# Another written order for the first part of an attention and two-MLP kernel

## The chip, the cores and the metric

The kernel runs on one core of a Trainium2 chip. The metric is the device time of one execution in microseconds (us). A core has five engines with instruction queues of their own: PE (matrix products; the load of its weights is shown as PEld), DVE (vector), ACT (functions such as exponential and sine), POOL (general purpose) and SP, whose queue issues the DMA transfers here. Each engine takes its queue strictly in order and waits on semaphores for the others.

## The reference, cut to what matters

```python
# attention: 4 batches, 8 heads, 576 positions, 64 columns
q_d, k_d, v_d = means of q, k, v over 4 neighbouring positions
out_d = softmax(scale * q_d @ k_d.T) @ v_d           # repeated 4 times
scores = scale * q @ k.T, only where |i - j| < 4     # a band of 7
x = repeat(out_d, 4) + softmax(scores) @ v           # -> 2304 x 512
# first MLP, d_ff 2048
h = x @ w_in;  y = (h * cos(h)) @ w_out
# second MLP, d_ff 1536
out = ((y @ w_a) * (y @ w_b)) @ w_out2
```

All is 32-bit floating point. The kernel splits each operand of a large product into a high and a low part and adds three products.

## The kernel before

The kernel has two parts. The first holds the attention, the first MLP and the preparation of the second MLP's weights; the second part is the second MLP. The change lies in the first part.

The 2304 positions are cut into eight half sequences u of 288. For each u the attention runs in two pairs of heads, pr 0 and 1. Its steps have short names, which the order and all the text below use with u and pr or a head pair behind: sm adds four neighbours of q and k (down_sums, L379, nine adds on POOL for sm0.x by sum4, L370, three reductions on DVE); lp and dp are the local and down-sampled scores on PE; lm is mask and row maximum on DVE; lu subtracts the maximum (L415); le and de are the exponentials on ACT (L442, L449); ln and dn the sums; lz and dz the scaling by them (L464, L486, on ACT L484); lt and dt the transposes on PE, lc and dc the copies behind them (L290, L292); da is the negation and maximum of the down-sampled scores (L436, L438); vp adds v on PE, vq copies it; at is the product with v; up and cb put both results together into x; xh and xl split x into its high and low part.

The first MLP follows block by block. hG.c are the matmuls of group G (one block of 128 hidden columns for one u) into PSUM for chunk c; cG.0 to cG.5 are six steps of h cos h (cosine, L653): c.0 on ACT, c.1 on DVE, c.2 the sine on ACT (L660), c.3 the product on DVE (L662), which also sets the PSUM buffer free, c.4 the copy of the high part and c.5 the low part (L668); bG.m are the matmuls back (three each, mm3, L587 to L589). wK.0 to wK.4 convert the K-th weight block (L266, L269, L271, L290 or L292, L580). Loads are L0.. for the first tensors and then Lq, Lk, Lv, Lw (sums of v, tile vs) and LcK (weight block K, L261); pN.0 is a load for the second MLP (praw).

What sets the order is one string, ORDER (L51 to L159), with 2320 words. Each word is a task; a letter behind @ names the engine (a ACT, d DVE, p POOL) where more than one can do it. The loop at L972 takes word after word and writes the task's instructions; the class InOrder (L175) then fixes for every engine that it keeps the written order. So a task's place in the string is its place in its engine's queue, and a load's place is its place in SP's queue. Buffers are few: att is one PSUM buffer, h is two, q tiles three; groups 2 and 3 use accumulators (EARLY). A load of a q tile waits until the tasks that read the buffer's last content are done, and everything behind it in SP's queue waits too. ACT holds one function table at a time: exponential and sine need different ones, and the build puts a table load (ACT_TABLE_LOAD, shown under the line of the instruction behind it) where the written order goes from one to the other.

Of the kernel before, what the change touches and what calls it, by code (L numbers as in the profile page):

```python
# [55 lines left out]
sm1.1@d Lc10 vq0.2@a ln0.1 lz0.1@d vq0.3@a Lc8 h0.0 w6.2@d h1.0 w9.1@a dz0.2@p dt0.1 dc0.1@a w3.0@a h1.1 Lq2.0 lt0.1 lc0.10@a lc0.11@a at0.1 w5.2@d
h2.0 h2.1 w6.3@d w10.1@a w9.2@d w3.1@a up0.1@d cb0.2 xh0.2@a cb0.3 w6.4@p w3.2@d h0.1 L0w7 sm1.0@d xh0.3@a xl0.3@d w8.1@a lp1.0 xl0.2@p h2.2 h1.2
w3.3@d h0.2 h0.3 w8.0@a w4.3@a w8.2@d w7.1@a lm1.0 c0.0@a w3.4@p Lc12 w4.4@p c0.1@d Lc15 Lk2.1 h1.3 c1.0@a c1.1@d Lc26 w7.0@a w7.2@d w7.3@d Lq1.2
w5.3@d h2.3 c2.0@a h3.0 h3.1 c0.2@a Lc13 h3.2 h3.3 c3.0@a dp1.0 c1.2@a dx1.0 w7.4@p Lq1.3 lu1.0@p c0.3@d da1.00@d c1.3@d lu1.1@d h5.0 h5.1 h5.2
da1.01@d sm1.2@d lp1.1 sm1.3@d w5.4@p c2.1@d Lk2.0 h4.0 Lc16 w12.0@a c0.4@d c1.4@d c1.5@p Lc27 w10.0@a w12.1@a w8.3@d Lc11 h4.1 lm1.1 h4.2 c0.5@p b0.1  # L60
w9.3@a h5.3 w10.2@d lu1.2@p le1.0 ln1.0 lz1.0@p de1.0 dn1.0 b0.0 Lc30 c2.2@a c3.1@d c2.3@d h4.3 dp1.1 dx1.1 da1.10@d w11.1@a c4.0@a Lc29 da1.11@d b1.0
lu1.3@p b0.3 b1.3 w8.4@d b1.1 dz1.0@p lt1.0 lc1.00@d lc1.01@d c3.2@a c3.3@d w9.4@d c2.4@a w13.0@a c2.5@p b2.0 b2.1 le1.1 dz1.1@p c3.4@d c3.5@p w15.1@a
dt1.0 ln1.1 dc1.0@a w10.3@a sm2.0@d b2.3 b0.2 w10.4@p b1.2 at1.0 b3.0 up1.0@d Lq2.1 c4.1@d w11.0@a cb1.1 c5.0@a b2.2 de1.1 b3.1 cb1.0 b3.3 dn1.1
lz1.1@p lt1.1 b3.2 c4.2@a Lw2.0 w11.2@d Lc18 lc1.11@a lc1.10@a Lc14 w11.3@a dz1.3@p sm2.1@d lp2.0 xh1.1@a c4.3@d c5.1@d lm2.0 vs2.0@p w15.0@a Lc24
xl1.1@d xh1.0@a w11.4@p h6.0 h6.1 Lc22 c4.4@a Lq2.2 dz1.2@p c5.2@a c5.3@d h6.2 Lc20 w14.1@a h6.3 c6.0@a w13.1@a lu2.1@p dt1.1 Lc19 dc1.1@d c5.4@a
c6.1@d w12.2@d c4.5@d h7.0 w14.0@a w12.3@a h7.1 at1.1 up1.1@a w14.2@d cb1.2 cb1.3 Lc25 c6.2@a c6.3@d h7.2 h7.3 c7.0@a xh1.2@a xh1.3@a xl1.0@p dp2.0
Lc21 w12.4@p b4.3 w13.2@d Lw2.1 Lk2.3 h8.0 w19.0@a b4.0 c7.1@d c7.2@a dx2.0 Lq2.3 c7.3@d w13.3@a h8.1 w20.1@a w20.0@a xl1.2@p h8.2 da2.00@d xl1.3@p
w15.2@d da2.01@d h9.0 h9.1 Lk2.2 h9.2 w27.0@a h9.3 vs2.1@p c6.4@a Lq3.0 lp2.1 c5.5@p h8.3 b4.1 w25.0@a w13.4@d b5.3 b5.1 sm2.3@d c6.5@p lm2.1 w14.3@a
w14.4@p Lc23 b4.2 b5.2 Lc17 b5.0 b6.0 lu2.0@p lu2.2@p c8.0@a c8.1@d w16.0@a Lc28 sm2.2@d c9.0@a c9.1@d b6.3 w24.0@a dp2.1 c8.2@a c8.3@d c7.4@d b6.1
lu2.3@p h10.0 w15.3@a w15.4@p dx2.1 da2.10@d h10.1 h10.2 c9.2@a le2.0 b6.2 Lv2 Lq3.2 da2.11@d h10.3 de2 c10.0@a c9.3@d c7.5@p b7.2 b7.0 ln2.0 Lw2.2  # L70
vs2.2@p h11.0 b7.1 le2.1 Lq3.1 lz2.0@p h11.1 c10.1@d c10.2@a dn2 h11.2 h11.3 c11.0@a c8.4@a c10.3@d b7.3 e7.0@d sm3.1@p e7.3@d lt2.0 dz2.0@p lc2.01@a
c11.1@d dz2.1@p h12.0 h12.1 h12.2 lc2.00@a dt2.0 Lw2.3 c8.5@p ln2.1 e7.2@a vs2.3@p c11.2@a c11.3@d c9.4@d h12.3 b8.2 dc2.0@a at2.0 w20.2@d up2.0@d
c12.0@a c12.1@d c9.5@p h13.0 w24.1@a w30.1@a S7.0 h13.1 c11.4@a lz2.1@p cb2.1 h13.2 h13.3 b8.0 b9.0 S7.2 c10.4@a c10.5@p sm3.0@d cb2.0 Lw2.4 vs2.4@p
w26.1@a e7.1@a c13.0@a S7.3 dp3.0 w24.2@d b8.1 b9.2 c13.1@d p1.0 dx3.0 da3.00@d da3.01@d c12.2@a w22.0@a b8.3 b9.3 b10.3 c13.2@a xh2.0@a lp3.0 xh2.1@a
c12.3@d Lw2.5 w20.3@a w16.1@a c13.3@d h14.0 h14.1 h14.2 w26.0@a w21.1@a c12.4@d dz2.3@a lm3.0 w16.2@d w30.0@a dz2.2@p h14.3 w20.4@p h15.0 lt2.1
lc2.10@a h15.1 lc2.11@d c14.0@a c11.5@d xl2.1@p w17.1@a w21.0@a h15.2 sm3.2@d h15.3 c15.0@a w24.3@d dt2.1 dc2.1@d lu3.1@p b9.1 Lq3.3 sm3.3@d c13.4@d
c12.5@d b10.1 c14.1@d b10.2 vs2.5@p Lq4.1 at2.1 b11.1 up2.1@d c15.1@d b10.0 w22.1@a c13.5@p cb2.2 w27.1@a b11.0 c14.2@a cb2.3 w17.0@a xh2.3@a b12.1
c14.3@d w27.2@d lu3.0@p b12.0 S7.1 lp3.1 xl2.3@d p1.11 Lk4.0 xh2.2@a xl2.0@p h16.0 lm3.1 w18.0@a b11.3 c15.2@a c15.3@d w22.2@d Lk4.1 c14.4@a xl2.2@p
w24.4@p le3.0 h16.1 b13.1 h16.2 dp3.1 dx3.1 w23.1@a c15.4@d da3.11@d da3.10@d h17.0 h17.1 Lv3 h17.2 h17.3 ln3.0 c14.5@p b14.1 c15.5@p w23.0@a b11.2
h16.3 w23.2@d c17.0@a de3 c17.1@d Lq4.3 b12.3 b13.3 b14.3 c16.0@a lz3.0@p c16.1@d w18.1@a dn3 c17.2@a b13.0 b14.0 b15.0 Lq4.0 w21.2@d lt3.0 c17.3@d  # L80
b12.2 lc3.01@a e15.0@a c16.2@a sm4.0@d b15.1 e15.1@a c16.3@d b13.2 b14.2 b15.2 e15.2@a w30.2@d lu3.2@p lc3.00@a b15.3 h19.0 w29.0@a h19.1 e15.3@a
h19.2 h19.3 c19.0@a c17.4@d Lw4.0 dz3.0@p S15.0 S15.2 sm4.1@d c16.4@a dz3.1@p dt3.0 dc3.0@a c19.1@d lu3.3@p h18.0 h18.1 c17.5@p h18.2 w17.2@d w19.1@a
at3.0 up3.0@d c16.5@p c19.2@a le3.1 vs4.0@p c19.3@d h18.3 b16.2 dz3.3@p h20.0 b16.3 cb3.1 Lw4.1 cb3.0 w19.2@d ln3.1 lz3.1@p c18.0@a c18.1@d b17.3
w19.3@a b16.1 w25.1@a dp4.0 vs4.1@p w22.3@a dx4.0 da4.01@d b16.0 b17.2 da4.00@d b17.1 S15.1 h20.1 w19.4@d c18.2@a c18.3@d h20.2 h20.3 c20.0@a dz3.2@a
lp4.0 c18.4@a c18.5@p b17.0 w22.4@d w27.3@a w27.4@p c20.1@d S15.3 lm4.0 lu4.1@p c20.2@a h21.0 h21.1 c19.4@a h21.2 h21.3 Lk4.2 Lq4.2 Lk4.3 c20.3@d
c21.0@a c19.5@p lu4.0@p b18.1 b18.2 b18.3 lt3.1 w16.3@a lc3.11@a h22.0 h22.1 w18.2@d c21.1@d lc3.10@a w16.4@d c21.2@a c21.3@d h22.2 w18.3@a c20.4@a
sm4.2@d dt3.1 Lq5.1 h22.3 b18.0 h23.0 b19.3 h23.1 h23.2 c22.0@a c22.1@d dc3.1@a h23.3 w21.3@a Lw4.2 vs4.2@d c22.2@a c22.3@d c23.0@a sm4.3@d b19.0
# [1183 lines left out]
```

## Time and profile before

| what | value |
|---|---|
| time, median of 3 runs (lowest to highest) | 895.76 us (895.41 to 896.43) |
| the profiled execution | 895.03 us, of which the span is 893.2 us |
| busy PE | 872.7 us, 98% of the span |
| busy DVE | 658.0 us, 74% |
| busy ACT | 551.5 us, 62% |
| busy POOL | 497.0 us, 56% |
| busy PE from 0 to 80 us | 63.06 us of 80 |
| moved by DMA | 162.10 MB, mean 181 GB/s |

The profile counts from the start of the span. A row of the timeline gives start and duration in us, the engine, the line, the instruction, what it writes from what, and in brackets how long the engine was idle before it and what ended that. The tables by stage give the busy time of each engine in a stretch with the count of instructions. The clock that PE was granted was at its full level in all stretches shown.

### The profile page before, as it was taken

To read this page: it belongs to the slowest core of one execution; us is meant where nothing else is said; L and a number is where in the kernel's file an instruction comes from. 1 tells how busy PE (TensorE), PEld (TensorE's weight loads), DVE (VectorE), ACT (ScalarE), POOL (GpSimd) and SP (SyncE) were. 2 spreads that over 40 slices of the span, in tenths; PEclk is the share of its full clock that TensorE was granted. 3 is DMA by queue.
4 is the path that set the end of the run, shared out by engine and by line. 5 is a ranking of instruction groups with operands and counts; after the bars stand their busy time and mean duration, and the time that the engine had idled before them with its cause. 6 is when DMAs were issued, how large, how long until landed. Compare 5 with 4: busy or idle time off the path is not lost.

```text
span 893.2 us, 17805 instructions
## 1 busy us (share of the span) xinstructions
PE 872.7 (98%) x6444; PEld 815.2 (91%) x6444; DVE 658.0 (74%) x1229; ACT 551.5 (62%) x1126; POOL 497.0 (56%) x656
## 2 busy tenths in 40 slices
...
GB/s 356 327 309 142 121 120 80 129 154 112 221 214 176 163 142 159 89 43 126 270 310 115 95 180 213 289 241 273 343 93 71 183 206 260 341 73 96 232 139 54
DMA packets 96935, 162.10 MB, mean 181 GB/s; under 512 B 6608, under 2 KB 64464, under 8 KB 96848
## 3 DMA queue, kind: packets, MB, share of 16 engines
...
## 4 chain that ended last, share of the span: by engine, by line
PE 93%; DMA 2%; DVE 2%; ACT 1%; POOL 1%; issue 1%; SPq 0%; POOLq 0%; ACTq 0%
PE z L587 15%; PE z L588 15%; PE z L589 15%; PE acc L587 8%; PE h L587 8%; PE acc L588 7%; PE acc L589 7%; PE h L588 7%; PE h L589 7%; PE att L398 1%; DMA raw<-in_w_in_dram 1%; PE att L422 1%; PE att L525 1%; DMA kq<-in_kq_dram 1%; PE att L493 1%; PE att L518 1%
## 5 line engine op out<-in xcount | busy, mean ns | idle before, releaser
L1006 POOL TENSOR_TENSOR sb<-w,sb 128x256 fp32r<-128x256 f32 x154 | 125.2, 825 | 121.0 <-ACT sb L1004 120.2
L1004 ACT ACTIVATE sb<-w 128x256 fp32r<-128x256 f32 x252 | 97.8, 415 | 51.6 <-PE z L589 43.4
L587 PE MATMUL h<-xbig,w 128*128 128x480 f32 (+3 forms) x352 | 128.1, 364 | 1.5 <-DVE gbig L662 1.5
L587 PE MATMUL acc<-tbig,w 128*128 128x480 f32 (+3 forms) x352 | 127.4, 362 | 0.5 <-DVE gbig L662 0.5
L588 PE MATMUL acc<-tbig,w 128*128 128x480 f32 (+3 forms) x352 | 124.5, 354 | 1.2 <-POOL tbig L668 1.2
L588 PE MATMUL h<-xbig,w 128*128 128x480 f32 (+3 forms) x352 | 124.2, 353 | 0.7 <-POOL xbig L560 0.7
L589 PE MATMUL acc<-tbig,w 128*128 128x480 f32 (+3 forms) x352 | 124.4, 353 | 0.1
L589 PE MATMUL h<-xbig,w 128*128 128x480 f32 (+3 forms) x352 | 124.0, 352 | 0.0
L668 POOL TENSOR_TENSOR tbig<-gbig,tbig 128x288 fp32r<-128x288 f32 (+3 forms) x47 | 51.7, 1102 | 96.5 <-ACT tbig L290 45.4
L656 ACT ACTIVATE gbig<-h,turn 128x480 int32<-128x480 f32 (+3 forms) x88 | 53.3, 607 | 69.7 <-PE h L589 63.9
L587 PE MATMUL z<-xbig,sb 128*128 128x384 f32 x288 | 96.2, 334 | 0.0
L589 PE MATMUL z<-xbig,sb 128*128 128x384 f32 x288 | 96.2, 334 | 0.0
L588 PE MATMUL z<-xbig,sb 128*128 128x384 f32 x288 | 96.2, 334 | 0.0
L658 DVE SCALAR_TENSOR_TENSOR gbig<-gbig,h 128x480 f32<-128x480 int32 (+3 forms) x88 | 51.3, 585 | 57.0 <-ACT gbig L656 56.5
L1006 DVE TENSOR_TENSOR sb<-w,sb 128x256 fp32r<-128x256 f32 x98 | 60.0, 614 | 21.8 <-ACT sb L1004 21.8
L587 PEld LDWEIGHTS h<-xbig,w 128*128 128x128 f32 x352 | 66.2, 188 | 10.5 <-DVE gbig L662 2.1
L587 PEld LDWEIGHTS acc<-tbig,w 128*128 128x128 f32 x352 | 66.2, 188 | 8.8 <-issue 1.5
L588 PEld LDWEIGHTS acc<-tbig,w 128*128 128x128 f32 x352 | 66.2, 188 | 7.8 <-POOL tbig L668 1.9
L588 PEld LDWEIGHTS h<-xbig,w 128*128 128x128 f32 x352 | 66.3, 188 | 6.8 <-POOL xbig L560 1.2
L589 PEld LDWEIGHTS acc<-tbig,w 128*128 128x128 f32 x352 | 66.1, 188 | 6.5 <-POOL w L580 0.3
L589 PEld LDWEIGHTS h<-xbig,w 128*128 128x128 f32 x352 | 66.2, 188 | 6.2
L660 ACT ACTIVATE gbig<-gbig,turn 128x480 f32<-128x480 f32 (+3 forms) x88 | 56.5, 644 | 22.9 <-DVE gbig L658 22.3
...
## 6 DMA issues: line engine op xcount, KB each, us to landing
...
```

Of the source, the lines that this page charges most:

```text
L398: pe.matmul(p[i][o, W * w:W * w + W], qt[u, 2 * pr + i][r, off:off + W], kt[u, 2 * pr + i][r, off:off + W], start=True, stop=True)
L422: pe.matmul(p[a][:QD, SD * i:SD * i + SD], qd[u, 2 * pr + i][r, :], kd[u // 2, 2 * pr + i][r, :], start=True, stop=True)
L493: pe.transpose(p[part][:, 128 * i:128 * i + 128], pt[u, pr][:, s], ident)
L587: i = pe.matmul(ps_out, lh, rh, start=start, stop=False, skip_group_check=more)
L588: pe.matmul(ps_out, lh, rl, start=False, stop=False, skip_group_check=more)
L589: pe.matmul(ps_out, ll, rh, start=False, stop=stop, skip_group_check=more)
L656: act.activation(out=gs[g].bitcast(I32), in_=hps[g], func=AF.Identity, scale=1.0 / (2.0 * math.pi), bias=turn[:, 0:1])
L658: dve.scalar_tensor_tensor(out=gs[g], in0=gs[g].bitcast(I32), scalar=-2.0 * math.pi, in1=hps[g], op0=ALU.mult, op1=ALU.add)
L660: act.activation(out=gs[g], in_=gs[g], func=AF.Sin, bias=turn[:, 1:2])
L668: eng.tensor_tensor(out=gl[g], in0=gs.pop(g), in1=gh[g].bitcast(F32), op=ALU.subtract)
L1004: act.activation(out=t[:, 0], in_=blk, func=AF.Copy)
L1006: (dve if nst[0] % (C["SD"] if G else C["SD0"]) == 0 else pool).tensor_tensor(out=t[:, 1], in0=blk, in1=t[:, 0].bitcast(F32), op=ALU.subtract)
```

## The change

Only the string ORDER changes. Its 2320 words are the same tasks; they stand in another order, and 213 of them name another engine, 48 of these in the part that before ran ahead of 100 us. The order of the tasks was searched with operation lengths drawn within a few per cent. The first line of each:

```diff
 ORDER = """
-L0k1 L0k0 lp0.0 sm0.0@p sm0.1@d dp0.0 L0w1 w1.0@a w1.1@a lm0.0 L0v0 L0k3 w1.2@d lu0.1@d L0V0 vp0.0 lu0.0@d dx0.0 L0w2 w1.3@d le0.0 ln0.0 lz0.0@d lt0.0
...
+L0k0 sm0.0@d L0k1 sm0.1@d lp0.0 lm0.0 L0w1 w1.1@a dp0.0 dx0.0 L0v0 w1.0@a da0.00@d lu0.0@p lu0.1@p le0.0 da0.01@d de0.0 L0w2 w2.1@a L0V0 vp0.0 w1.2@d
...
```

The first place is the head of DVE's queue, behind its constants. The two rows with L373 are one down sum each time, L405 and L410 the maximum lm0.0, L271 the weight step w1.2, and L415 the subtractions lu0.1 and lu0.0. Before:

```order
L373 TENSOR_REDUCE kd<-kq 128x72 x2
L373 TENSOR_REDUCE qd<-kq 128x72
L405 TENSOR_TENSOR smx<-att,mask 128x2x5x64
L410 TENSOR_REDUCE mx<-smx 128x10
L271 SCALAR_TENSOR_TENSOR raw<-raw 128x512
L415 TENSOR_TENSOR smx<-smx,mx 128x5x64 x2
L428 TENSOR_REDUCE mxd<-att 72x2 x2
```

After:

```order
L373 TENSOR_REDUCE kd<-kq 128x72 x2
L373 TENSOR_REDUCE qd<-kq 128x72
L373 TENSOR_REDUCE kd<-kq 128x72 x2
L373 TENSOR_REDUCE qd<-kq 128x72
L405 TENSOR_TENSOR smx<-att,mask 128x2x5x64
L410 TENSOR_REDUCE mx<-smx 128x10
L428 TENSOR_REDUCE mxd<-att 72x2 x2
L438 TENSOR_TENSOR smd<-mxd,att 72x2x3x48 x2
L271 SCALAR_TENSOR_TENSOR raw<-raw 128x512
```

DVE now does both first down sums (sm0.0 came from POOL), the subtractions L415 are gone to POOL, and the maximum and the negations of the down-sampled scores stand ahead of w1.2.

The second place is ACT's queue about the exponentials of u = 1: le1.0 and le1.1 are the rows L442, de1.0 is L449, the sines are L660, the copies into tbig are c.4. Before, from le1.0's table load to le1.1:

```order
L442 ACT_TABLE_LOAD
L442 ACTIVATE smx<-smx 128x640
L449 ACTIVATE smd,sd<-smd 72x3x48 x4
L660 ACT_TABLE_LOAD
L660 ACTIVATE gbig<-gbig,turn 128x288
L269 ACTIVATE raw<-raw,turn 128x512
L656 ACTIVATE gbig<-h,turn 128x288
L660 ACTIVATE gbig<-gbig,turn 128x288
L290 ACTIVATE tbig<-gbig 128x288
L266 ACTIVATE raw<-raw 128x512
L442 ACT_TABLE_LOAD
L442 ACTIVATE smx<-smx 128x640
```

After, the same stretch:

```order
L442 ACT_TABLE_LOAD
L442 ACTIVATE smx<-smx 128x640
L290 ACTIVATE tbig<-gbig 128x288
L266 ACTIVATE raw<-raw 128x512
L290 ACTIVATE tbig<-gbig 128x288
L656 ACTIVATE gbig<-h,turn 128x288
L269 ACTIVATE raw<-raw,turn 128x512
L449 ACTIVATE smd,sd<-smd 72x3x48 x4
L656 ACTIVATE gbig<-h,turn 128x288
L290 ACTIVATE w<-raw 128x512 x2
L442 ACTIVATE smx<-smx 128x640
```

The sines c2.2 and c3.2 that stood between the two exponentials now stand ahead of le1.0; one table load stands in this stretch where there were three. In the new order the row L656 is c5.0 and the row L269 behind it w11.1.

The third place is SP's queue about q2.1. The row with L311 is a load of a q tile, L816 the load p1.0, L327 a load of vs, L261 of weight blocks. Before; c11 is the last of the three loads from in_w_in:

```order
L311 DMA q<-in_qT_dram 128x292
L299 DMA k<-in_kT_dram 128x292 x2
L261 DMA raw<-in_w_in_dram 128x512 x3
L261 DMA raw<-in_w_out_dram 128x512 x2
L311 DMA q<-in_qT_dram 128x292
L327 DMA vs<-in_vds_dram 128x512
```

After:

```order
L261 DMA raw<-in_w_out_dram 128x512
L311 DMA q<-in_qT_dram 128x292
L816 DMA praw<-in_w_a_dram 128x512
L327 DMA vs<-in_vds_dram 128x512
L261 DMA raw<-in_w_in_dram 128x512
L299 DMA k<-in_kT_dram 128x292 x2
```

The load of c11 (the first L261 with in_w_in behind L327) now stands behind q2.1, p1.0 and a vs load; it stood ahead of q2.1.

## Rows read from the trace of the kernel before

**Rows 1.** Busy time by stretches: start:end, length, PE, PEld, DVE, ACT, POOL, clock, DMA.

```profile
0.00:20.00 20.00, 10.15 (x198) 8.65 (x202) 13.25 (x34) 11.78 (x29) 14.94 (x36) 1.00 0.91 350
20.00:40.00 20.00, 16.17 (x263) 14.02 (x255) 19.22 (x43) 19.60 (x43) 13.01 (x12) 1.00 0.87 318
40.00:60.00 20.00, 17.29 (x248) 15.07 (x249) 18.37 (x47) 19.88 (x45) 15.82 (x19) 1.00 0.88 339
60.00:80.00 20.00, 19.45 (x238) 17.87 (x237) 19.37 (x43) 19.51 (x37) 17.65 (x25) 1.00 0.59 196
80.00:100.00 20.00, 19.99 (x332) 18.50 (x333) 18.59 (x42) 18.34 (x39) 15.49 (x23) 1.00 0.54 162
```

**Rows 2.** PE's waits: what it waited for, us in total, times, longest.

```profile
PE att L398 <- DMA kq<-in_kq_dram: 5.3, 1, 5.3
```

**Rows 3.** Timeline of the head, several engines.

```profile
5.36 0.31 POOL L375 TENSOR_TENSOR kd<-kq 128x72 f32<-128x72 f32 x1 [0.43 <-DMA kq<-in_kq_dram]
...
6.81 0.82 DVE L405 TENSOR_TENSOR smx<-att,mask 128x640 f32<-128x640 f32 x1 [1.51 <-PE att L398]
...
8.96 1.24 PE L422 MATMUL att<-kd,qd 64*72 64x144 f32 x8 [2.30 <-POOL qd L377]
9.09 0.69 DVE L271 SCALAR_TENSOR_TENSOR raw<-raw 128x512 uint32<-128x512 uint32 x1 [0.60 <-ACT raw L269]
...
10.75 0.74 ACT L442 ACTIVATE smx<-smx 128x640 f32<-128x640 f32 x1 [1.69 <-DVE smx L415]
```

**Rows 4.** Timeline of ACT's table loads, first and last of five, and lp2.0.

```profile
36.05 1.28 ACT L660 ACT_TABLE_LOAD   x1
...
41.09 1.28 ACT L442 ACT_TABLE_LOAD   x1
...
42.38 0.74 ACT L442 ACTIVATE smx<-smx 128x640 f32<-128x640 f32 x1
...
54.47 1.28 ACT L660 ACT_TABLE_LOAD   x1
...
57.01 0.91 PE L398 MATMUL att<-k,q 64*64 64x64 f32 x40 [0.77 <-ACT smx L290]
```

**Rows 5.** Timeline of c0.3 on DVE and h5.0 on PE.

```profile
38.00 0.44 DVE L662 TENSOR_TENSOR gbig<-gbig,h 128x288 f32<-128x288 f32 x1
...
38.49 0.40 PE L587 MATMUL h<-xbig,w 128*128 128x288 f32 x1 [1.32 <-DVE gbig L662]
```

**Rows 6.** Groups by form, 0 to 100 us; the third row: min/median/max by tile.

```profile
L373 DVE TENSOR_REDUCE kd<-kq 128x72 f32<-128x288 f32 x4 | 1.6, 441 | 1.6 <-DMA kq<-in_kq_dram 1.6
L415 DVE TENSOR_TENSOR smx<-smx,mx 128x320 f32<-128x320 f32 x5 | 2.5, 529 | 0.0
L415 POOL TENSOR_TENSOR smx<-smx,mx x9: 719/737/1042, 38.5 to 96.7; 128x320 f32<-128x320 f32 x9
L464 DVE TENSOR_TENSOR smx<-smx,sl 128x640 f32<-128x640 f32 x2 | 1.8, 908 | 0.1
L464 POOL TENSOR_TENSOR smx<-smx,sl 128x640 f32<-128x640 f32 x4 | 5.0, 1259 | 0.7 <-DVE sd L476 0.7
L290 ACT ACTIVATE w<-raw 128x512 fp32r<-128x512 f32 x10 | 6.8, 676 | 0.2 <-DVE raw L271 0.2
L290 ACT ACTIVATE tbig<-gbig 128x288 fp32r<-128x288 f32 x7 | 2.9, 433 | 0.0
L290 ACT ACTIVATE smx<-att 128x384 f32<-128x384 f32 x5 | 2.4, 482 | 0.7 <-PE att L493 0.7
L436 ACT ACTIVATE smd<-att,mxd 72x144 f32<-72x144 f32 x6 | 1.8, 373 | 0.0
L484 ACT ACTIVATE smd<-smd,sd 72x144 f32<-72x144 f32 x2 | 0.7, 399 | 0.0
```

**Rows 7.** SP's issue of weight loads, and their time to landing, 0 to 70 us.

```profile
34.99 1.39 SPq L261 DMA_DIRECT2D raw<-in_w_in_dram  x3
DMA to landing us min/median/max: 4.3/8.2/9.3
```

212 lines of the change are left out of this document (106 added, 106 removed).

## The prediction

> **What bounds the kernel now.** I read the table of busy time by stage first [rows 1]. The reader is to see that PE, which carries the matmuls, has gaps in the first 80 us alone: 10.15, 16.17, 17.29 and 19.45 us busy of 20 each, so 16.9 us idle. The page puts PE at 98% of the span, and the second part runs on a full PE. So an order of the first part can act only through those 16.9 us. In the same rows ACT is busy 19.60, 19.88 and 19.51 us from 20 to 80 us: in this stretch it, not PE, is the full engine. DVE follows with 19.22, 18.37 and 19.37. POOL has room.
>
> Next the list of PE's waits [rows 2]: the largest, 5.3 us, is the first load, which the change leaves first in the queue (k0 and k1 change places, and both stand before anything else). The waits that a reordering can touch are then the end of the first down sums on POOL (2.30 us, at 8.96) [rows 3], ACT's copy lc1.10 ahead of lp2.0 (0.77 us, at 57.01) [rows 4] and the cosine step c0.3 on DVE (1.32 us, at 38.49) [rows 5].
>
> Third the timeline of the head [rows 3]. POOL spends the time from 5.36 until PE goes on at 8.96 on nine small adds (sm0.0), while DVE sits idle 1.51 us until the local scores arrive. ACT's first exponential le0.0 starts at 10.75 because DVE does w1.2 (0.69 us, which itself waits for ACT) before the two subtractions lu0.1 and lu0.0. From 10.75 on, ACT hardly stops: it is the queue that carries an early lead or delay through to lp2.0.
>
> Last, ACT's own rows [rows 4]: each change between exponential and sine brings a table load of 1.28 us. Up to lp2.0 there are five, the first at 36.05 and the last at 54.47, together 6.4 us on the full engine.
>
> **The change part by part.** All sums are made against the profiled execution, 895.03 us (span 893.2), which is 0.73 below the median of 895.76; I take the difference found there off the median.
>
> *Head, down sums.* sm0.0 goes from POOL to DVE: nine adds that took 3.6 us become three reductions, by the mean form 3 x 0.44 = 1.3 us at most [rows 6], and they go into the 1.51 us in which DVE waits. dp0.0 can start at about 6.8 instead of 8.96. This 2.2 us isn't a gain by itself, because the next thing PE needs, lt0.0, hangs on le0.0.
>
> *Head, subtractions.* lu0.0 and lu0.1 go to POOL. It is free by then, since its nine adds are gone. lm0.0, an instruction of 0.82 us from 6.81 [rows 3] and a second of that length, ends at 8.5. Two subtractions on POOL took between 0.72 and 1.04 us each elsewhere, 0.74 in the median [rows 6]: they end between 9.9 and 10.6, while le0.0 started at 10.75. The lead of le0.0 is thus between 0.1 and 0.8 us. I take 0.6, nearer to the median. lz0.0 on POOL costs 1.26 instead of 0.91 us [rows 6], so lt0.0 keeps 0.25 of it; ACT has other work before it copies lt0.0's result and should keep all.
>
> On two engines reading at once the row shows that POOL's subtraction is slower than DVE's (0.74 against 0.53 [rows 6]) and nothing of who blocked whom. The Trainium skill, "SBUF — State Buffer", section "SBUF: two separate sides", says that a DVE operation with two SBUF inputs and a GpSimd operation that reads SBUF hold a shared port exclusively, so that the later one stands still for a whole instruction. By that rule w1.2 on DVE would stop lu0.1 or lz0.0 for its 0.69 us, and le0.0's lead would be about nothing.
>
> *Table loads.* In the new order the sines c0.2 to c3.2 stand together, then le1.0, de1.0 and le1.1, then c4.2. So ACT has three loads ahead of lp2.0 and not five: 2 x 1.28 = 2.57 us less.
>
> The rows show nothing else at a switch: the exponential behind the load of 41.09 starts at 42.38, a hundredth after its end. The Trainium skill, "ScalarE: Activation LUTs", section "What ACT_TABLE_LOAD costs", gives 1283 ns for the load, which agrees with these rows, and about 1380 ns more for a drain, which they don't show; by its full figure the term would be 5.3 us instead of 2.57.
>
> *Work moved onto ACT ahead of lp2.0*, by the mean of each form [rows 6]: two c.4 copies +0.87; dz0.0, two scalings, +0.80; w6.3 +0.68; one lc copy more +0.48; two negations (da) of two pieces each fewer, -1.49. xh0, dc0.0 against dc0.1, and w14.0 against w13.0 cancel. Sum +1.34. So ACT's queue is 2.57 - 1.34 = 1.23 us shorter at lp2.0.
>
> *DVE.* Ahead of c5.3, which releases h7.0, stand 118 of these tasks' instructions before and after. The order of PE's work ahead of h7.0 holds the same groups. So DVE's queue is as long as it was, but 1.1 to 1.3 us of it lies in the hole at 5.3 us. Ahead of c0.3 there are 73 against 67 instructions: six short ones more eat the 1.1 us again at that place, so h5.0 keeps its wait of 1.3 us [rows 5] or most of it, and the lead comes only behind it.
>
> *The waits after that.* c0.5 no longer holds b0.1, because other matmuls (h5.3, h4.0 to h4.3) come first; lp2.0 is then released by ACT. Its lead is 0.6 + 1.2 = 1.8 us, from 57.0 to 55.2. Between 60 and 80 us PE was idle 0.55 us [rows 1]; DVE, which released those waits, has its 1.1 us from the hole, so I take this off too. I see nothing that is late next: from 80 to 100 us PE stands 0.01 us [rows 1]. The second part and the other 165 engine changes lie behind a full PE and cost nothing; without that cover one of them would cost what a POOL form costs above DVE's, 0.35 us for lz.
>
> Sum: 0.6 + 1.23 + 0.55 = 2.4 us. The low end is 0.6: half of DVE's hole, should DVE pace and not ACT. The high end is 4.1: the idle time that ACT still has from 20 to 80 us (0.40 + 0.12 + 0.49 = 1.0) goes as well, and 0.7 more of the 2.2 at dp0.0 is kept.
>
> **The rivals.**
> *A, DVE paces.* DVE has as much work ahead of h7.0 as it had. If it paces, the gain is what of the filled hole it doesn't wait later on ACT and PE, between half and all: 0.6 to 1.2 us, 894.6 to 895.2. For it: DVE is busy 18.4 to 19.4 of 20 us. Against it: ACT is the fuller of the two in all three rows.
> *B, all leads add.* 4.1 us, 891.7. For it: DVE, ACT and PE (dp0.0, by 2.2 us) each start earlier. Against it: the smallest of the three leads is what an in-order PE gets.
> *C, slower: the load queue.* In the new order SP's load of q2.1 stands ahead of p1.0 (an early weight of the second part), a vs load and c11. q2.1 waits for sm1.1, which stands on DVE five tasks of about 0.5 us ahead of c0.3 (at 38.00 before [rows 5]) and ends between 35.4 and 36.5; c11, in a group issued from 34.99 before [rows 7], would go out at about 37.5. Its conversion w11.1 stands on ACT four short tasks behind le1.0, which ended at 43.1 [rows 4]; 1.2 us earlier and four tasks of 0.43 to 0.68 us later, that is 43.8. Loads of this line took 4.3 to 9.3 us to land, 8.2 in the median [rows 7]: c11 is there between 41.8 and 46.8. At the late end ACT stands 3.0 us, all of the gain and 0.6 us more: 896.4. It turns slower from a landing at 46.2; beyond 897.6 it comes from 48.0, that is if DVE also gives q2.1 free 1.2 us later. Against it: while q2.1 holds the queue the loads ahead drain, so c11 has little before it and should land in the first half of that spread.
>
> *D, the port.* If a DVE operation stops one of POOL's for its whole length, le0.0 gains nothing (0.6 less) and lz0.0 loses one more stop as long as w1.2, 0.69 us [rows 3]: 2.4 - 0.6 - 0.69 = 1.1 us, 894.7. The rows show only that POOL's times spread (0.72 to 1.04), by less than such a stop.
>
> The rule that the Trainium skill states in "SBUF — State Buffer", "SBUF: two separate sides", is the one by which D would come.
>
> **How the numbers follow.** A measurement of this kernel can tell about 0.2%, 1.8 us, from no change: faster is below 893.96, slower above 897.56. Forecast (a gain of 1.8 to 3.3 us): 0.50, predicted at 895.76 - 2.4 = 893.4. B 0.14. A 0.20 and D 0.06, both within 0.2%. C 0.10, of which 0.06 beyond 0.2% and 0.04 within. So faster 0.64, same 0.30, slower 0.06. The range from 891.7 (B) to 895.2 (the low end of A) leaves out C and the tail of B, about 0.15.
>
> **What would show it.** dp0.0 on PE at about 6.8; le0.0 on ACT at about 10.1 (10.75 before); three table loads on ACT ahead of lp2.0; lp2.0 at about 55.2 and h7.0 about 2 us earlier too; PE busy more than 17.29 us of 20 between 40 and 60, by one to two; no wait of ACT for a load between 40 and 50 us; no PE gap that is new before 36 us. A lp2.0 at 56 or later means A or D; a wait of w11.1 means C. A PE gap after 100 us would make the frame wrong.

## The result and the profile after

The changed kernel takes 903.59 us in the median of 6 runs (903.1 to 905.23) against 895.76 of 6 runs of the kernel before (894.8 to 896.57): ratio 1.0089, 95% interval 1.0076 to 1.0102. It is 7.8 us slower where 2.4 us less was forecast. The profiled execution took 903.1 us, its span is 901.4 (before 893.2).

| what | before | after |
|---|---|---|
| busy PE | 872.7 us, 98% | 876.0 us, 97% |
| busy DVE | 658.0 us | 666.6 us |
| busy ACT | 551.5 us | 547.8 us |
| busy POOL | 497.0 us | 502.6 us |
| bytes moved | 162.10 MB | 162.10 MB |

The same tables by stage as [rows 1], of after, and below them the stretches behind 100 us in which PE is not full; the columns are those of [rows 1]:

```profile
0.00:20.00 20.00, 10.73 (x220) 8.76 (x221) 14.94 (x42) 12.77 (x37) 10.68 (x22) 1.00 0.92 354
20.00:40.00 20.00, 16.83 (x232) 14.28 (x231) 19.47 (x42) 19.55 (x35) 12.62 (x14) 1.00 0.64 226
40.00:60.00 20.00, 16.42 (x244) 14.23 (x244) 17.43 (x40) 17.55 (x44) 17.16 (x20) 1.00 0.99 376
60.00:80.00 20.00, 19.21 (x231) 17.15 (x229) 18.47 (x41) 17.79 (x35) 18.09 (x21) 1.00 0.76 252
80.00:100.00 20.00, 19.74 (x298) 18.41 (x298) 18.19 (x40) 18.98 (x38) 17.05 (x26) 1.00 0.43 123
...
100.00:150.00 50.00, 48.11 (x563) 44.55 (x562) 47.54 (x92) 43.67 (x80) 36.68 (x40) 1.00 0.34 107
...
250.00:300.00 50.00, 48.69 (x471) 39.42 (x470) 39.12 (x75) 34.29 (x58) 30.04 (x57) 1.00 0.69 212
...
350.00:400.00 50.00, 48.85 (x284) 41.86 (x283) 23.06 (x41) 19.53 (x30) 11.17 (x18) 1.00 0.22 66
...
450.00:500.00 50.00, 49.62 (x227) 42.13 (x226) 33.36 (x47) 23.15 (x43) 18.21 (x17) 1.00 0.60 198
```

The row of before for the 400 us behind 100 us:

```profile
100.00:500.00 400.00, 400.00 (x2941) 351.78 (x2940) 273.11 (x497) 242.95 (x421) 186.77 (x288) 1.00 0.48 152
```

The reader is to see three things. The first two rows are better than before, by 0.58 and 0.66 us of busy PE. From 40 to 60 us PE lost 0.87 us and ACT 2.33. And behind 100 us, where before shows 400.00 us busy of 400, PE now stands in four stretches.

How far PE has come can't be read from busy time alone, since the orders differ. So every PE instruction gets a price by its form (what it writes from what, and the shape). Consecutive instructions of one form make a run; a run's time to the next start, divided by its instructions, is its pace, and the price is the best pace of that form in the two traces. The prices of all instructions started up to a time t are summed and taken off t. The result is how far PE is behind a PE that always keeps this pace:

| t (us) | 25 | 40 | 50 | 60 | 80 | 100 | 125 | 250 | 280 | 350 | 370 | 450 | 500 |
|---|---|---|---|---|---|---|---|---|---|---|---|---|---|
| before | 19.2 | 23.7 | 27.0 | 29.1 | 31.2 | 33.2 | 34.5 | 39.7 | 40.9 | 43.7 | 44.0 | 45.0 | 46.0 |
| after | 18.1 | 23.0 | 26.0 | 29.1 | 32.1 | 34.3 | 38.3 | 43.8 | 47.2 | 49.6 | 51.3 | 52.3 | 54.0 |
| after less before | -1.0 | -0.7 | -1.0 | 0.0 | +0.9 | +1.1 | +3.8 | +4.1 | +6.3 | +5.8 | +7.3 | +7.3 | +8.0 |

The lowest row is taken before rounding. The two upper rows hang on the choice of price, the lowest hardly: with the median pace instead of the best it changes by at most 0.4 us. Ahead of 25 us the measure isn't used, since the two orders have done different work there and the difference hangs on the price.

Behind 500 us some 0.2 us are added; 8.2 us is the difference of the spans. So a lead of about 1 us was there from 25 to 50 us, it was gone at 60, and the rise comes in steps: 1.1 us from 60 to 100, 2.7 up to 125, 2.2 at 250 to 280, 1.5 at 350 to 370, 0.7 behind 450.

The head, as [rows 3] to [rows 5], in the timeline of after (start, duration, engine, line, instruction, idle before it):

```profile
6.57 1.24 PE L422 MATMUL att<-kd,qd 64*72 64x144 f32 x8
...
8.53 1.41 POOL L415 TENSOR_TENSOR smx<-smx,mx 128x320 f32<-128x320 f32 x2 [3.59 <-DVE mx L410]
...
9.97 0.75 ACT L442 ACTIVATE smx<-smx 128x640 f32<-128x640 f32 x1 [1.60 <-POOL smx L415]
...
35.51 1.28 ACT L660 ACT_TABLE_LOAD   x1
...
37.88 0.40 PE L587 MATMUL h<-xbig,w 128*128 128x288 f32 x1 [0.89 <-DVE gbig L662]
...
39.35 1.28 ACT L442 ACT_TABLE_LOAD   x1
...
49.79 0.76 ACT L269 ACTIVATE raw<-raw,turn 128x512 uint32<-128x512 uint8 x1 [1.75 <-DMA raw<-in_w_out_dram]
...
51.28 0.56 PE L505 MATMUL att<-ident,smd 72*112 72x72 f32 x6 [1.62 <-ACT smx L290]
...
54.25 1.28 ACT L660 ACT_TABLE_LOAD   x1
...
57.28 0.81 PE L398 MATMUL att<-k,q 64*64 64x64 f32 x40 [0.52 <-ACT smx L290]
```

The head came as forecast: dp0.0 at 6.57, le0.0 at 9.97, three table loads ahead of lp2.0, h5.0's wait kept in good part. Then ACT stood 1.75 us at 49.79, at w15.1, until the load of c15 was there, and lp2.0 came at 57.28 and not at 55.2. SP's queue in after shows when that load was issued:

```profile
35.28 0.33 SPq L311 DMA_DIRECT2D q<-in_qT_dram  x1
35.65 0.43 SPq L816 DMA_DIRECT2D praw<-in_w_a_dram  x1
36.13 0.43 SPq L327 DMA_DIRECT2D vs<-in_vds_dram  x1
36.60 0.43 SPq L261 DMA_DIRECT2D raw<-in_w_in_dram  x1
...
39.82 0.56 SPq L261 DMA_DIRECT2D raw<-in_w_out_dram  x1
```

The last row is c15, issued 10.0 us before ACT had it and 8.2 before ACT was ready for it, behind q2.1, p1.0, a vs load and five more; DMA was 0.99 busy from 40 to 60 us (0.88 before [rows 1]). This wait is in the one profiled execution of after, and experiment 3 shows that it isn't in others with the same order.

The largest step, at 110 to 117 us, in the timeline of after, DVE's rows first, then POOL's, ACT's and PE's:

```profile
111.65 2.65 DVE L271 SCALAR_TENSOR_TENSOR raw<-raw 128x512 uint32<-128x512 uint32 x1
...
116.13 0.68 DVE L271 SCALAR_TENSOR_TENSOR raw<-raw 128x512 uint32<-128x512 uint32 x1
...
111.19 1.29 POOL L486 TENSOR_TENSOR smd<-smd,sd 72x288 f32<-72x288 f32 x2 [0.40 <-DVE sd L477]
112.44 1.31 POOL L580 TENSOR_TENSOR w<-raw,w 128x512 fp32r<-128x512 f32 x1
...
114.80 0.38 ACT L290 ACTIVATE smx<-att 128x256 f32<-128x256 f32 x1 [1.95 <-DVE smx L292]
...
115.33 0.56 PE L505 MATMUL att<-ident,smd 72*112 72x72 f32 x6 [1.29 <-ACT smx L290]
```

w18.2 on DVE takes 0.68 us as a rule (second row) and took 2.65 here: it begins beside POOL's two scalings dz3.1 and dz3.0 and ends just behind POOL's next operation, w24.4 (112.44 + 1.31 = 113.75). The copy lc3.00 stands behind it on DVE, ACT waits for that, PE for ACT.

Two more steps have one pattern, a conversion of the second part's weights that stands in its engine's queue ahead of the landing of its load; in after's timeline DVE, PE, ACT and PE again:

```profile
268.20 0.69 DVE L271 SCALAR_TENSOR_TENSOR praw<-praw 128x512 uint32<-128x512 uint32 x1 [2.17 <-ACT praw L269]
268.81 0.60 DVE L292 COPY smd<-att 112x432 f32<-112x432 f32 x1
...
273.90 0.74 PE L493 MATMUL att<-ident,smx 128*128 128x128 f32 x5 [1.06 <-DVE xf L538]
...
358.10 0.67 ACT L266 ACTIVATE praw<-praw 128x512 f32<-128x512 f32 x1 [2.34 <-DMA praw<-in_w_b_dram]
...
360.09 0.49 PE L587 MATMUL h<-xbig,w 128*128 128x480 f32 x1 [1.15 <-DVE gbig L662]
```

At 268 DVE stands 2.17 us for ACT's conversion of p9, which began at 266.79, as its load landed (issued at 261.58, 5.1 us to landing); the copy dc6.0 is in DVE's queue behind; PE waits at lt6.1 (L493) for DVE's additions L538, which come later by that. At 358 ACT stands 2.34 us at p23.10, and the sine c60.2 stands behind it, whose result DVE's L662 and then h62.0 need.

### The profile page after: what moved, and what is told of

Its sections match the earlier page's. It is cut to its first block, busy times and chain, and to the rows that moved or that the text cites. A ratio compares the mean times of both kernels' runs of the same rounds, so it can differ in the third digit from the quotient of the medians.

```text
span 901.4 us, 17798 instructions
## 1 busy us (share of the span) xinstructions
PE 876.0 (97%) x6444; PEld 814.9 (90%) x6444; DVE 666.6 (74%) x1236; ACT 547.8 (61%) x1121; POOL 502.6 (56%) x637
## 2 busy tenths in 40 slices
DMA packets 96935, 162.10 MB, mean 180 GB/s; under 512 B 6608, under 2 KB 64464, under 8 KB 96848
## 4 chain that ended last, share of the span: by engine, by line
PE 80%; DMA 7%; DVE 6%; POOL 2%; ACT 2%; issue 2%; SPq 1%; DVEq 0%; POOLq 0%; ACTq 0%
PE z L588 15%; PE z L589 15%; PE z L587 15%; PE acc L587 6%; PE acc L588 6%; PE acc L589 6%; PE h L587 5%; PE h L589 5%; PE h L588 5%; DMA k<-in_kT_dram 2%; DMA raw<-in_w_in_dram 1%; DMA praw<-in_w_a_dram 1%; DMA kq<-in_kq_dram 1%; DMA praw<-in_w_b_dram 1%; PE att L398 1%
## 5 line engine op out<-in xcount | busy, mean ns | idle before, releaser
L668 POOL TENSOR_TENSOR tbig<-gbig,tbig 128x288 fp32r<-128x288 f32 (+3 forms) x53 | 57.2, 1084 | 71.5 <-DVE tbig L292 36.7
L656 ACT ACTIVATE gbig<-h,turn 128x480 int32<-128x480 f32 (+3 forms) x88 | 53.2, 605 | 48.5 <-PE h L589 42.9
L658 DVE SCALAR_TENSOR_TENSOR gbig<-gbig,h 128x480 f32<-128x480 int32 (+3 forms) x88 | 51.1, 582 | 38.3 <-ACT gbig L656 37.7
L660 ACT ACTIVATE gbig<-gbig,turn 128x480 f32<-128x480 f32 (+3 forms) x88 | 56.1, 642 | 33.6 <-DVE gbig L658 32.9
```

What stands on the lines that cost most here:

```text
L656: act.activation(out=gs[g].bitcast(I32), in_=hps[g], func=AF.Identity, scale=1.0 / (2.0 * math.pi), bias=turn[:, 0:1])
L658: dve.scalar_tensor_tensor(out=gs[g], in0=gs[g].bitcast(I32), scalar=-2.0 * math.pi, in1=hps[g], op0=ALU.mult, op1=ALU.add)
L660: act.activation(out=gs[g], in_=gs[g], func=AF.Sin, bias=turn[:, 1:2])
L668: eng.tensor_tensor(out=gl[g], in0=gs.pop(g), in1=gh[g].bitcast(F32), op=ALU.subtract)
```

## The experiments

Times are medians; the number with a sign is the difference to the kernel before, measured beside it (895.8 to 896.8 us), the brackets hold the 95% interval of the ratio. After itself is at +7.8, 1.0089 [1.0076, 1.0102]. The diffs show the words of the order around each edit.

**1. Which half carries it.** a1_order has the new order with every task on its old engine, a2_engines the old order with the new engines:

```diff
-L0k0 sm0.0@d L0k1 sm0.1@d lp0.0 lm0.0 L0w1 w1.1@a dp0.0 dx0.0 L0v0 w1.0@a da0.00@d lu0.0@p lu0.1@p le0.0
+L0k0 sm0.0@p L0k1 sm0.1@d lp0.0 lm0.0 L0w1 w1.1@a dp0.0 dx0.0 L0v0 w1.0@a da0.00@a lu0.0@d lu0.1@d le0.0
```

> The new written order with the old engine of every task. Theory O (the loss comes from the places in the queues, loads among them): it keeps most of the loss, 901 to 904 us, and PE's gaps about 50, 113, 272 and 359 us stay. Theory E (the loss comes from the engines, DVE and POOL standing in each other's way): it is close to before, 895 to 897 us, and the 2.65 us operation on DVE at 111.65 is gone.

```diff
-L0k1 L0k0 lp0.0 sm0.0@p sm0.1@d dp0.0 L0w1 w1.0@a w1.1@a lm0.0 L0v0 L0k3 w1.2@d lu0.1@d
+L0k1 L0k0 lp0.0 sm0.0@d sm0.1@d dp0.0 L0w1 w1.0@a w1.1@a lm0.0 L0v0 L0k3 w1.2@d lu0.1@p
```

> The old written order with the new engine of every task. Theory O: close to before, 895 to 898 us. Theory E: 901 to 904 us. If both a1 and a2 lose several us, the two only fit together as they were searched.

Measured: a1_order 961.58 (+64.8, ratio 1.0726 [1.0708, 1.0744]), a2_engines 929.04 (+32.2, 1.0364 [1.0349, 1.0380]). The ranges of both expectations failed by far; what came is the case in the last sentence of a2's, that both lose. Busy time from 100 to 500 us in a1_order:

```profile
100.00:500.00 400.00, 367.27 (x2952) 318.10 (x2951) 251.69 (x466) 228.14 (x397) 180.18 (x284) 0.97 0.40 122
```

And the same in a2_engines:

```profile
100.00:500.00 400.00, 384.98 (x3011) 334.54 (x3010) 276.68 (x500) 239.21 (x416) 197.22 (x286) 1.00 0.47 144
```

PE stands 32.7 and 15.0 us in a stretch in which before has no wait at all. So the full PE of before is no property of the stage with room to spare: it holds for this order with these engines. Neither mixture was searched as a whole, so their size doesn't rank the two halves.

**2. Which stage carries it.** a3_head_new follows the new order up to lp2.0 and then the old, a4_head_old the other way round; each is shown at its cut, against after and before:

```diff
 b3.2 sm2.1@d lp2.0
-lm2.0 c5.2@a c5.3@d Lc20 h6.0 h6.1 w11.3@a
+Lc26 Lc30 Lc29 w13.0@a w11.3@a xh1.1@a lm2.0
```

> The new order and engines up to and with lp2.0, then all other tasks as before. By the traces the new head is 1.7 us ahead at 20 us and has lost all of it by 60 us, so if the loss after 60 us belongs to the later part: 895 to 897 us. If the new head leaves a debt that shows only later (loads issued late): 899 us or more.

```diff
 dz1.3@p sm2.1@d lp2.0
-xh1.1@a c4.3@d c5.1@d lm2.0 vs2.0@p w15.0@a Lc24
+p1.0 w14.0@a Lc25 c5.1@d Lc28 Lc19 Lc23
```

> The old order and engines up to and with lp2.0, then the new ones. If the later part alone carries the loss: 902 to 905 us, with the gaps about 113, 272 and 359 us. If the loss is a debt of the new head: 895 to 898 us.

Measured: a3_head_new 896.80 (0.0, 1.0001 [0.9992, 1.0011]), a4_head_old 902.33 (+5.5, 1.0075 [1.0048, 1.0103]). The first has 400.00 us of busy PE from 100 to 500 us, the second 395.00 (after: 395.27). So the later part of the new order carries most of the rise, 5.5 of 7.8 us (its four runs spread from 901.32 to 906.71); the new head, followed by the old order, neither gains nor costs.

**3. The places one by one.** b1_load sets three loads (Lw2.0 is the one of vs) behind that of c15:

```diff
-w7.1@a Lq2.1 w7.2@d
+w7.1@a w7.2@d
...
-h3.1 p1.0 c0.2@a c0.3@d dp1.0 h3.2 h3.3 c3.0@a Lw2.0 c3.1@d
+h3.1 c0.2@a c0.3@d dp1.0 h3.2 h3.3 c3.0@a c3.1@d
...
-Lc15 c1.5@p
+Lc15 Lq2.1 p1.0 Lw2.0 c1.5@p
```

> The changed kernel with three loads (q2.1, p1.0 and a vs load) moved behind the load of c15 in SP's queue, all else as it is. Theory Q (the head's lead is lost at 48 to 50 us because ACT stands 1.75 us for c15): that wait goes, lp2.0 comes 1.0 to 1.7 us earlier, and the time is 901.9 to 902.6 us. Theory R (DVE or POOL would have lost it there anyway): the wait goes, but the time stays at 903 to 904 us.

Measured: 902.06 (+6.1, 1.0068 [1.0055, 1.0081]), 1.7 less than after, with an interval that overlaps after's. w15.1 in the timeline of its ACT, the row behind L266:

```profile
47.81 0.66 ACT L266 ACTIVATE raw<-raw 128x512 f32<-128x512 f32 x1
48.37 0.78 ACT L269 ACTIVATE raw<-raw,turn 128x512 uint32<-128x512 uint8 x1
```

No wait is left, and lp2.0 came at 56.15. But the traces don't show that this is the edit's doing. Six more kernels have after's order up to lp2.0, these loads included (a3_head_new, b2_w18, b3_prep, c1_pool, c2_poolq, c3_prep2), and in none of their profiled executions does w15.1 wait. The row in c1_pool:

```profile
47.91 0.78 ACT L269 ACTIVATE raw<-raw,turn 128x512 uint32<-128x512 uint8 x1
```

There c15 was issued at 39.15 instead of 39.82, with DMA as busy (0.99 from 40 to 60 us). So the late load is seen in one execution of seven, and where b1_load's 1.7 us come from is not shown: by the measure of the table above its profiled execution (902.75) is 0.9 us ahead of before at 57 us, level at 100 and 8.0 behind at the end.

b2_w18 and c1_pool go at the stall of 110 us, by DVE's and by POOL's order:

```diff
-w18.2@d dz3.2@a lz3.0@p lt3.0 lc3.00@d c16.2@a c16.3@d sm4.0@d
+dz3.2@a lz3.0@p lt3.0 lc3.00@d c16.2@a c16.3@d w18.2@d sm4.0@d
```

> The changed kernel with one DVE task, w18.2, written behind c16.3 instead of ahead of lc3.00. Theory P (that operation took 2.65 us because POOL was reading at the same time, and lc3.00 and c16.3, which read the matmul's buffer, don't suffer so): PE's gap about 113 us is gone, 901 to 902 us. Theory N (DVE is held up there whatever stands first, for instance by something that blocks the engine itself): lc3.00 or c16.3 takes long in its place, and the time stays at 903 to 904 us.

```diff
-w23.2@d w24.4@p dt3.0 dc3.0@a Lv3 c16.5@p c17.4@a c17.5@p h18.0
+w23.2@d dt3.0 dc3.0@a Lv3 c16.5@p c17.4@a c17.5@p w24.4@p h18.0
```

> The changed kernel with one POOL task (w24.4, a subtraction of 1.3 us that ran beside the long w18.2) written later, behind c17.5; DVE's queue is as it was. Theory P (w18.2 stood still while POOL worked): w18.2 shortens from 2.65 to about 1.4 us, ending with POOL's two scalings before it, dt3.0 comes 1.2 us earlier, 902.2 us where after gave 903.6. Theory N (DVE is held for another reason): 2.65 us as before, 903.6 us.

Measured: b2_w18 901.88 (+5.9, its five runs spread from 898.41 to 903.63), c1_pool 900.88 (+4.9, 1.0057 [1.0043, 1.0070]), 2.9 less than after. The same operations in c1_pool, DVE and POOL:

```profile
110.05 0.75 DVE L271 SCALAR_TENSOR_TENSOR raw<-raw 128x512 uint32<-128x512 uint32 x1
...
109.58 1.74 POOL L486 TENSOR_TENSOR smd<-smd,sd 72x288 f32<-72x288 f32 x2 [0.40 <-DVE sd L477]
```

With one POOL operation taken from behind the pair w18.2 is back at 0.75 us, and now POOL's pair is longer, 1.74 for 1.29; the wait of dt3.0 is gone. Of the two one stands for the other. This place is no chance of one execution: w18.2 takes 2.64 to 2.66 us in all six traces that have this stretch as after has it (after, a4_head_old, b1_load, b3_prep, c2_poolq, c3_prep2), and by the table's measure these lose 2.7 to 3.2 us from 100 to 125 us, c1_pool 1.5. That is 1.2 of c1_pool's 2.9 us; its profiled execution was 1.8 us ahead of after's already at lp2.0 (55.45 against 57.28). In b2_w18 lc3.00 took its usual 0.54 us, but w18.2 still 1.63 us at its new place, and PE's wait moved to another matmul (1.50 us at 117.96, for DVE's L662).

b3_prep and c3_prep2 set the conversions of p9 and p23 later, the first by much, the second only behind the copies that they held (p23 as in the last two lines of the second diff in both):

```diff
-p9.10 dz6.3@p b44.1 p9.11 p9.12 p9.2 dt6.0
+dz6.3@p b44.1 dt6.0
...
-xh6.0@a xl5.3@d
+xh6.0@a p9.10 p9.11 p9.12 p9.2 xl5.3@d
```

> The changed kernel with the conversions of two weights of the second part written later: p9 (four tasks) behind xh6.0 and p23 (two tasks) behind c60.3. Theory Q (ACT and DVE stand in order behind conversions whose load isn't there yet): the gaps about 272 and 359 us go, together 2.5 us, 901 to 901.5 us. If the gaps are DVE's own load: 903 to 904 us.

```diff
-b44.1 p9.11 p9.12 p9.2 dt6.0 dc6.0@d p8.5
+b44.1 dt6.0 dc6.0@d p9.11 p9.12 p9.2 p8.5
...
-p23.10 c60.2@a p23.11 cb7.3 b57.1 c60.3@d b57.2
+c60.2@a cb7.3 b57.1 c60.3@d p23.10 p23.11 b57.2
```

> The changed kernel with p23's two conversions behind c60.3 and the p9 tasks one place later, behind dc6.0 (in the run before, p9's four tasks went much later and held back the next weight loads). Theory Q (in-order engines stand behind a conversion whose load isn't there): the gap about 359 us goes (1.3 us), that about 272 shrinks by 0.5, 901.7 to 902.3 us. Otherwise 903 to 904 us.

Measured: b3_prep 910.26 (+14.3), c3_prep2 901.71 (+5.7, 1.0071 [1.0055, 1.0087]), 2.1 less than after. In c3_prep2 DVE's wait of 2.17 us is down to 1.02 and ACT's of 2.34 to 0.82. b3_prep missed: the loads of the next weights wait for the buffer that p9 holds, so later work was late instead. A store of converted weights that went out at 270.83 in after went out at 277.60, the load behind it at 282.36 (274.43), and ACT stood 8.07 us for that load. PE in b3_prep:

```profile
278.25 0.97 PE L505 MATMUL att<-ident,smd 72*112 72x72 f32 x6 [2.66 <-POOL smd L486]
...
290.03 0.81 PE L398 MATMUL att<-k,q 64*64 64x64 f32 x40 [2.37 <-issue]
```

c2_poolq changes POOL's order between 60 and 100 us:

```diff
-vs2.1@p c5.5@p c6.4@a c6.5@p
+c5.5@p c6.4@a c6.5@p vs2.1@p
...
-vs2.3@p dc2.0@a
+dc2.0@a
...
-sm3.0@p dp3.0
+sm3.0@p vs2.3@p dp3.0
```

> The changed kernel with two POOL tasks put back in POOL's queue: vs2.1 behind c6.5 and vs2.3 behind sm3.0, so that c5.5 and sm3.0, which PE waits for, go first. Theory L (from 60 to 90 us POOL is the engine that is late, since tasks were moved onto it): PE's gaps at b5.2 (0.85 us) and dp3.0 (0.42 us) go, 902.3 us. If DVE or ACT is as late as POOL there: 903 to 904 us.

Measured: 905.52 (+9.5, 1.0104 [1.0091, 1.0118]), worse than after. PE's waits for others in c2_poolq from 60 to 105 us (what waited, for whom, total, times, longest):

```profile
PE acc L589 <- POOL w L580: 1.4, 1, 1.4
PE att L505 <- ACT smx L290: 1.0, 1, 1.0
```

The two waits aimed at are gone and these stand in their place, the first again for POOL, the second over ACT for a copy on DVE. So POOL's order alone doesn't help. POOL is busy 18.09 + 17.05 us of 40 there in after, and was 17.65 + 15.49 [rows 1].

**4. Do the losses add up?** b4_all has the edits of b1_load, b2_w18 and b3_prep:

> The three edits together. If each gap is a loss of its own, they add: 896.5 to 899 us. If one only uncovers the next: 900 us or more.

It took 909.13 (+13.2), close to the +14.3 of b3_prep, whose edit it holds; so it can't tell whether the losses add. d1_three has the edits of b1_load, c1_pool and c3_prep2, d2_five two places more:

> The changed kernel with three moves at once: the loads of w_in's q and praw tasks (q2.1, p1.0) and of the next layer weights behind the load of c15; w24.4 on POOL behind c17.5, so that DVE's w18.2 does not stand still beside it; the weight conversions p9.11, p9.12, p9.2 behind dc6.0 and p23.10, p23.11 behind c60.3. Theory that the losses are separate and add: 903.6 less 1.5 (as the load alone gave), less 2.7 (w24.4 alone), less 1.9 (the conversions alone), so 897.5, between 896.5 and 898.5. Rival, that each repair only uncovers the next late thing on an engine with no room: 899.5 or more, with gaps on PE at other places than the ones removed.

```diff
-vs2.1@p c5.5@p c6.4@a c6.5@p sm2.3@d w24.0@a
+c5.5@p c6.4@a c6.5@p sm2.3@d w24.0@a
...
-w14.4@p lu2.2@p
+w14.4@p vs2.1@p lu2.2@p
...
-p29.3 p29.4 x9.4
+p29.3 x9.4
...
-b76.3 p32.4 p32.5 c78.4@a
+b76.3 c78.4@a
...
-c80.3@d c79.4@d
+c80.3@d p32.4 p32.5 c79.4@d
...
-c81.3@d x9.1
+c81.3@d p29.4 x9.1
```

> As d1_three, with two more moves: vs2.1 on POOL behind w14.4 (the gap at b5.3, 0.85 us), and p29.4 behind c81.3, p32.4 and p32.5 behind c80.3 (the gap at 455 to 469 us, 0.8 to 0.9 us). Theory of separate losses: 1.0 to 2.0 us below d1_three, so 895.4 to 896.5 if d1_three is at 897.5. Rival, that POOL is late between 60 and 100 us whatever its order, as the move of vs2.1 and vs2.3 alone gave no gain: within 0.6 us of d1_three, with the gap of b5.3 come back as one at b6.3 or dt2.1.

Measured: d1_three 898.94 (+2.6, 1.0028 [1.0018, 1.0038]), d2_five 899.85 (+3.5, 1.0041 [1.0026, 1.0055]). Singly the three edits took 1.7 + 2.9 + 2.1 = 6.7 us off; together 5.2. So together they account for two thirds of the rise. By the table's measure 3.2 us of that are seen where c1_pool and c3_prep2 edit: after loses 2.7 us from 100 to 125 us and 3.2 from 250 to 370, d1_three's trace 1.4 and 1.3. b1_load's share has no place that shows it. The two more moves gave nothing, nearly as the rival said (0.9 us above d1_three where it allowed 0.6): in d2_five the wait at b5.3 is gone, one of 0.76 us at 76.54 is new, and dp3.0 waits 1.3 us for POOL's qd.

**5. Can the head's lead be kept?** c4_cut27 and d3_cut68 follow the new order up to at0.1 and up to lp2.1 (this one with b1_load's edit), and then the old:

```diff
 lc0.10@a at0.1
-w6.3@a h2.0 w3.0@a w9.2@d up0.1@d Lc10 cb0.2
+Lq1.1 sm1.1@d Lc10 Lc8 w3.0@a Lq2.0 h2.0
```

> The new order and engines only up to and with at0.1 (27 us), then all as before. By the traces the new head is there 0.8 to 1.7 us ahead. If that lead can be kept by the old rest: 894.2 to 895.2 us. If the old rest was paced by something else from there on: 895.7 to 896.5 us.

```diff
 w14.3@a h9.3 lp2.1
-w15.2@d h8.2 h8.3 vs2.1@p c5.5@p c6.4@a c6.5@p
+Lc26 Lc30 w19.0@a w20.1@a h8.2 w15.2@d w27.0@a
```

> The changed order and engines (with the loads behind that of c15) up to lp2.1, and from there those of the kernel before. Theory that the head's lead is real and is only spent later: TensorE comes to lp2.1 some 1.1 us ahead of the kernel before, is full from there on as before, and the time is 894.9 (894.3 to 895.4). Rival, that the lead is borrowed from work which the old order needs done by then (so it was at the two other cuts, at 17 and at 57 us): 896 to 897, with new gaps on PE right behind the cut.

Measured: c4_cut27 896.05 (+0.1, 0.9998 [0.9989, 1.0007]), d3_cut68 897.39 (+1.0, 1.0006 [0.9998, 1.0015]). The lead doesn't last at any cut: by the table's measure it is 1.0 us at 25 us in c4_cut27, 0.5 at 30 and 0.2 at 40; in d3_cut68 it is 0.7 at 57 us, and at 80 PE is 0.6 behind.

In most profiles of the new head PE's granted clock falls, to 1.2 from 2.4 GHz. The table by stretches of d1_three, ahead of the fall and at it:

```profile
12.00:14.00 2.00, 0.26 (x2) 0.26 (x3) 1.93 (x9) 2.00 (x7) 1.57 (x2) 1.00 1.02 403
...
16.00:18.00 2.00, 1.70 (x64) 1.53 (x56) 1.16 (x5) 2.00 (x6) 1.54 (x2) 0.50 1.01 401
```

And after in the same two stretches, where it stayed:

```profile
12.00:14.00 2.00, 0.51 (x5) 0.51 (x5) 1.97 (x8) 2.00 (x5) 1.82 (x2) 1.00 1.01 404
...
16.00:18.00 2.00, 1.08 (x56) 0.87 (x49) 1.75 (x6) 2.00 (x5) 1.54 (x2) 1.00 1.02 408
```

The share 0.50 held from 16 to 26 us in d1_three. Of 81 runs of the kernel before beside these kernels, the 22 at a mean clock of 1.000 took 894.55 to 895.83, the 57 at 0.998 or less 895.63 to 898.2. The two lowest runs of b2_w18 (898.41 and 898.53) and of d1_three (896.51 and 897.47) are those at 1.000 as well. Hence the next theory: PE's waits in the head cost it the clock, and the clock the lead. Three kernels fill these waits with transposes of the identity whose result nothing uses: e1_warm_cut is c4_cut27 with them, e2_warm_before the kernel before, e3_warm_three is d1_three.

```diff
+    def warm(tag, n):
+        t = ps.tile([128, 512], F32, tag=tag, name="warm", bufs=1)
+        for _ in range(n):
+            pe.transpose(t[:, :128], ident, ident)
...
+    warms = {"lt0.0": ("acc0", 10), "h0.0": ("acc2", 8), "dt0.1": ("acc2", 10)}
...
+            if key in warms:
+                warm(*warms[key])
```

> The head of the changed kernel up to at0.1, the rest as before (c4_cut27), with 28 transposes of the identity matrix added on PE where it waits in the head: 10 ahead of lt0.0, 8 ahead of h0.0, 10 ahead of dt0.1. Their results are used by nothing. Theory that the lead of the new head is lost because PE's waits in it (1.7, 1.1 and 1.8 us in the trace of c4_cut27) are followed by 3 us at a granted clock of 0.50: with the waits filled the granted clock is 1.00 throughout, and the time is 893.8 (893.3 to 894.6), some 1.2 below the 895.0 of executions of the kernel before at a mean clock of 1.000. Rival, that the added work stands in the way of what waited, or that the clock falls all the same: 895.5 to 897.

(e2_warm_before: `{"lp0.1": ("h", 10), "vp0.1": ("h", 12)}`.)

> The kernel before, with 22 transposes of the identity matrix added on PE: 10 ahead of lp0.1 and 12 ahead of vp0.1, where the trace of before shows PE idle for 1.38 and 1.56 us. It is the mate of e1_warm_cut. Theory: the executions of before at a mean clock under 1.000 take 896.0 to 897.2, those at 1.000 take 895.0, so with the waits filled all take 895.0 (894.6 to 895.8), and e1_warm_cut stays about 1.2 below. Rival, that the clock of this head falls for another reason: 896.0 to 896.4 in the median, as without them.

> d1_three (the changed kernel with three repairs) with the same 28 transposes as e1_warm_cut. Theory that of d1_three's 898.9 about 1.5 to 2.4 us are the lower clock in the head (its two executions at a mean clock of 1.000 took 896.5 and 897.5), so that the three repairs did add up: 896.5 to 897.5. Rival, that the repairs only uncover the next late thing whatever the clock: 898.5 to 899.5.

Measured: e1_warm_cut 895.44 (-0.4, 0.9996 [0.9987, 1.0005]), e2_warm_before 896.21 (+0.4, 1.0003 [0.9994, 1.0012]), e3_warm_three 898.68 (+2.9, 1.0035 [1.0023, 1.0048]). In all 27 runs of the three the mean clock was 1.000 or 0.999: PE's waits are what lowered it. The times did not follow. e2_warm_before has runs at 895.08 to 895.47 and at 896.21 to 897.15, all at that clock, as wide as without the transposes. In e1_warm_cut the lead is 1.0 us at 30 us and nothing at 35, at the full clock: there the old rest takes it back, not the clock. So the clock goes with the slower executions and isn't what makes them slower by this test, with one reserve: the transposes themselves stood in the way (dt0.1 began at 26.27 in e1_warm_cut, at 25.83 in c4_cut27), and all five runs of e3_warm_three lie above the two of d1_three at 1.000, so what they cost in all is open.

e3_warm_three also answers for the rest of d1_three. At 60 us it is 1.1 us ahead of the kernel before by the measure of the table above, so the head's lead was there; it then loses 0.8 us up to 100, 1.4 up to 125, 1.9 from 250 to 280 and ends 3.8 behind.

## Why the prediction was wrong

- **The head's steps held.** dp0.0 was put at about 6.8 and came at 6.57; le0.0's lead, taken as 0.6 from a range of 0.1 to 0.8, was 10.75 - 9.97 = 0.78; the two subtractions took 1.41 us on POOL, so 0.71 each where 0.72 to 1.04 was the range. Table loads ahead of lp2.0: three, as said. The exponential behind the load of 39.35 starts at 40.65, 0.02 us behind its end, so no drain is seen after the change either.
- **lp2.0 at 55.2** was right where neither a load nor the clock was in the way: with the same head it came at 55.45 in c1_pool and at 55.36 in b2_w18. In the profiled execution of after it was 57.28, behind the load; in the four others with this order of loads, with the clock down in the head, 56.57 to 57.92.
- **Rival C named the mechanism and not the load.** It put q2.1, p1.0 and vs ahead of c11 and had ACT stand at w11.1. c11 was in time; c15, issued at 39.82 where c11 was at 36.60, was not. Its price was put at up to 3.0 us, 1.75 was measured on ACT. The step "the loads ahead drain" didn't hold in that execution: DMA was 0.99 busy from 40 to 60 us. But ACT had no such wait in the six others with these loads, so this isn't what made the median.
- **The waits from 60 to 80 us** were to give 0.55 us. They grew: 0.9 us were lost up to 80 and 0.2 up to 100. The step "POOL has room" is at fault, which the prediction gives without a number: in this stretch POOL was busy 17.65 of 20 [rows 1], the change put work on it (18.09), and PE's longest wait there, 0.58 us at 71.11, is for POOL's L668. That POOL's load is the cause is argued from these waits; no run took the work off again.
- **The step that decided** is "The second part and the other 165 engine changes lie behind a full PE and cost nothing", with "I see nothing that is late next". A full PE in the trace of before says that there nobody was late, not by how much. The table of busy time has no column for that room, and a new order doesn't inherit it. a1_order and a2_engines showed how little there is, a4_head_old that most of the loss sits there. Of the 8.2 us between the spans about 7 are lost behind 100 us, where the sum has nothing. The price set for the case, 0.35 us for one POOL form above DVE's, was that of an operation's length; what came were whole waits in a queue, which set PE back by 0.7 to 2.7 us each.
- **Rival D, the port.** It was put into the head at 0.69 us a stop and had DVE stop POOL. In the head neither of the two stops is seen (w1.2 took 0.69 us, lz0.0 1.26). At 111 us it was the other way round, DVE's w18.2 stood for POOL, and cost 2.65 - 0.68 = 2.0 us. The Trainium skill, "SBUF — State Buffer", section "SBUF: two separate sides", calls the shared port "an exclusive lock, not a bandwidth split", which whichever starts first holds for its whole instruction. The trace agrees on the lock, and c1_pool shows either side standing; it shows more than one instruction's stop too, since w18.2 ended at 114.30, behind the end of POOL's next operation at 113.75 as well.
- **The test that the prediction set for itself**, "a PE gap after 100 us would make the frame wrong", is the one that it failed.

What stays open: of the rise d1_three leaves 2.6 us (2.9 with the transposes). PE's waits that are left are known (b5.3, b6.3 and dp3.0, all behind POOL; h18.2 and lp4.0; the stretch at 460), not an order that removes them. Nor is it settled why the same head executes in one run without and in another with waits at h0.0 and w15.1, where b1_load's 1.7 us come from, nor why executions of the kernel before differ by 1 to 2 us once the clock is held. No version ran that beats the kernel before by more than the interval.
